# An attention and MoE chain on one core: the reciprocals are spread to the partitions in two transfers for each pair of heads

## The chip, the core and the metric

The kernel runs on one core of a Trainium2 chip. The metric is the device time of one execution in microseconds (us), as the median of several runs. One more execution was recorded by the hardware profiler; the views below are of it.

The core has five engines that run side by side, each in its own order of instructions: TensorE (PE in the views, PEld for its weight loads), VectorE (DVE), ScalarE (ACT), GpSimd (POOL) and SyncE (SP). All transfers of this kernel are issued by SP and carried by 16 DMA engines.

## The reference

Three parts follow one another. The first is a linear attention over 4 batches, 8 heads, 576 positions and 64 channels:

```
phi(x):  proj = x @ w_phi;  proj -= max(abs(proj));  concat(exp(proj), exp(-proj))
kv  = phi(k)^T v            z   = sum over s of phi(k)
num = phi(q) kv             den = phi(q) z + 1e-6
attn = num / den
```

The second is `h = x @ w_in; g = max(0.01 h, h); g @ w_out` on 2304 tokens with 512 and 2048 channels. The third is a mixture of four experts, `sum over e of p_e * (max(x @ w1_e, 0) @ w2_e)`, with normalized probabilities `p`.

## The kernel before

Heads are worked on in pairs (`hp`), so that two heads of 64 channels fill 128 partitions; a batch has four pairs. For each pair a list of steps is put out (`STEPS`, line 385): loads of `k`, `q` and `v` (lines 154, 161, 166), the features of `k` (`k_feat`), the product with `v` (`kv_side`), the projection of `q` and its absolute maximum over the partitions by GpSimd (`q_proj`, line 296, tile `mb`), the subtraction (`q_sub`, line 301), the exponentials (`q_exp`, tile `e`) and the numerator (`q_num`, line 335, copied to `nf` by ScalarE). In `nf` one row also carries the denominators, since `v` is extended by ones.

Three steps then divide. `x_den` (line 347) takes the row of denominators of each head by a small transfer to a tile `ds` of 128 partitions and 9 columns (line 352). `x_rec` (line 357) adds 1e-6 and takes the reciprocal on VectorE (lines 359 and 360), writes the 2 x 576 values to a DRAM tile `dr` (line 362), and reads them back into a tile `rb` of 128 x 576 in which each of the two rows is repeated over 64 partitions (line 364). `x_mul` (line 367) multiplies each head's half of `nf` with its half of `rb` into `xr` (line 378), and splits `xr` into a rounded part `xh` on ScalarE and a rest `xl` on VectorE (lines 117 and 118).

The second part of the reference works in units of 128 of the 2048 channels (`moe1_up`, `moe1_down`). Its matmuls need all four pairs of a batch. In the first batch the weights are also taken apart from 64 bit words: loads of 1 MB for two units (`w64_dma`, line 442), then a split by one ScalarE and several VectorE instructions (`w64_split`, lines 457 to 464 and 118), and a write of the result to DRAM (line 468) for the later batches, which load it back (line 432). The third part follows from about 650 us on.

The attention of batch `b + 1` is woven between the second part's steps of batch `b` by a table of due times (`TIMES`, with `LO` and `HI`); the first batch's attention comes ahead of everything. The order in which these functions are called isn't the final one. A scheduler orders the instructions of each engine by its own estimate of when each would be ready, up to the third part, whose instructions are kept in program order (`kept`). SP's queue too is ordered in this way. An instruction of an engine, SP's issues included, doesn't start before the one ahead of it on that engine.

Of the kernel before, what the change touches and what calls it, by code (L numbers as in the profile page):

```python
# [14 lines left out]
B, H, S, D = 4, 8, 576, 64  # L15
# [64 lines left out]
def body(ctx, tc, kT, qT, vh, w_phi, w_in, w_out, probs, w1, w2, out):  # L80
    nc = tc.nc
# [22 lines left out]
    def unit(name, dt=F32):  # L104
        return up.tile([128, S], dt, tag="u", name=name)
# [251 lines left out]
    def x_rec(b, hp):  # L357
        ds = dss[b, hp]
        nc.vector.tensor_scalar(out=ds, in0=ds, scalar1=1e-6, scalar2=None, op0=ALU.add)
        nc.vector.reciprocal(ds, ds)  # L360
        dr = drp.tile([2, S], F32, tag="dr", name="dr")
        nc.sync.dma_start(out=dr.rearrange("a (p c) -> (a p) c", c=9), in_=ds)
        rb = unit("rb")
        nc.sync.dma_start(out=rb, in_=dr.unsqueeze(1).to_broadcast([2, D, S]))
        dss[b, hp] = rb

    def x_mul(b, hp):
# [41 lines left out]
        (q_num, 1, (1,)),  # L409
        (x_den, None, ()),  # L410
        (x_rec, None, ()),
        (x_mul, None, ()),
    )
# [521 lines left out]
```

## Time and profile before

| | |
|---|---|
| median of 3 runs | 1399.87 us (1398.96 to 1400.92) |
| profiled execution | 1398.86 us, span 1397.1 us |
| TensorE busy | 1355.4 us, 97% |
| VectorE busy | 816.9 us, 58% |
| ScalarE busy | 658.4 us, 47% |
| GpSimd busy | 572.7 us, 41% |
| transfers on the hardware queue | 133.58 MB, 29.2% of 16 engines' span |

How to read the views. The page gives busy times and shares, and the span in 40 slices of about 35 us as digits (tenths). The table by stretches has a line for each stretch: its bounds in us, its length, then for PE, PEld, DVE, ACT and POOL the busy time and in brackets the number of instructions, then TensorE's granted clock as a share of 2.4 GHz, the mean share of the 16 DMA engines that is busy, and the rate in GB/s. The time line has the start in us, the duration in us, engine, line, operation, output and inputs, shapes, the number of instructions merged into the row, and in square brackets how long the engine sat idle before and what ended that. A row of SP is the issue of a transfer, not the transfer. The list of transfers gives the size of each kind.

### The profile page before, as it was taken

What the parts mean: (1) busy time and instruction counts of PE and PEld (TensorE: products, weight loads), DVE (VectorE), ACT (ScalarE), POOL (GpSimd) and SP (SyncE); (2) the same over time, 40 slices, a digit from 0 to 9 for tenths busy, and PEclk for the clock granted to TensorE, in tenths of its full rate; (3) what the DMA queues carried; (4) which work ended last, traced back from release to release, by engine and by line L of the source; (5) the groups of instructions that cost most, each with busy time, mean ns of one, the idle gap of its engine ahead of it and who ended that gap; (6) DMA issues with size and microseconds to landing.
All of it is one profiled execution on the core that took longest, in us unless ns stands there. A gap on an engine that the chain in (4) does not pass through costs nothing.

```text
span 1397.1 us, 21274 instructions
## 1 busy us (share of the span) xinstructions
PE 1355.4 (97%) x8105; PEld 1264.4 (91%) x8105; DVE 816.9 (58%) x1285; ACT 658.4 (47%) x1201; POOL 572.7 (41%) x398
## 2 busy tenths in 40 slices
PE   8769989999999999999999999999999999999998
PEld 6668989999999999998999899999999999999997
DVE  5359879877777566554454544454445544454445
ACT  5547755676566544433344433444344333333331
POOL 3123101111111000015676675667677675656551
PEclk9979999999999999999999999999999999999999
DMA  6348554333332232222211221321212131212111
GB/s 218 95 120 299 199 201 126 124 107 102 113 102 78 78 105 79 69 69 76 76 61 61 76 69 67 112 70 61 76 62 74 61 119 63 76 61 76 61 61 61
DMA packets 78038, 134.94 MB, mean 97 GB/s; under 512 B 11760, under 2 KB 22128, under 8 KB 77936
## 3 DMA queue, kind: packets, MB, share of 16 engines
q1 hardware_dynamic: 77936, 133.58, 29.2%
q8 instruction: 64, 1.05, 0.3%
q14 instruction: 38, 0.31, 0.1%
HBM read 120.30 MB, written 13.18 MB: 96 GB/s over the span
## 4 chain that ended last, share of the span: by engine, by line
PE 86%; DMA 6%; DVE 4%; issue 2%; ACT 1%; POOL 0%; SPq 0%; DVEq 0%; ACTq 0%; POOLq 0%
PE po L758 28%; PE op L535 13%; PE hp L503 12%; PE py L719 11%; PE pv L719 7%; PE px L719 7%; PE kvp L242 4%; PE nm L335 2%; DMA rb<-dr 2%; DMA qraw<-qT 2%; PE pk L204 2%; DMA w<-w 1%; DMA r<-w_in 1%; PE pq L292 1%; DVE w L461 1%
## 5 line engine op out<-in xcount | busy, mean ns | idle before, releaser
L758 PE MATMUL po<-wd,gh 128*128 128x512 f32 x1152 | 387.4, 391 | 0.9 <-POOL wd L711 0.9
L774 DVE SCALAR_TENSOR_TENSOR ob<-po,pe,ob 128x512 f32<-128x512 f32 x270 | 201.6, 749 | 216.5 <-PE po L758 216.5
L758 PEld LDWEIGHTS po<-wd,gh 128*128 128x128 f32 x1152 | 216.3, 188 | 42.5 <-POOL wd L711 1.3
L535 PE MATMUL op<-gt,wt 128*128 128x288 f32 x1536 | 222.7, 299 | 6.7 <-DVE g L517 5.3
L296 POOL PARTITION_ALL_REDUCE mb<-pc x32 | 76.9, 2406 | 370.8 <-ACT pc L294 312.6
L758 PE MATMUL po<-wd,gl 128*128 128x512 f32 x576 | 226.0, 392 | 0.0
L503 PE MATMUL hp<-xh,wt 128*128 128x288 f32 x1024 | 216.1, 298 | 3.3 <-ACT xh L117 3.3
L535 PEld LDWEIGHTS op<-gt,wt 128*128 128x128 f32 x1536 | 210.3, 190 | 8.4 <-DVE g L517 5.8
L503 PEld LDWEIGHTS hp<-xh,wt 128*128 128x128 f32 x1024 | 167.5, 188 | 4.3 <-ACT xh L117 3.6
L503 PE MATMUL hp<-xl,wt 128*128 128x288 f32 x512 | 152.2, 297 | 0.4 <-DVE xl L118 0.4
L711 POOL TENSOR_TENSOR wd<-r,wd 128x1024 fp32r<-128x1024 f32 x48 | 115.1, 2397 | 88.8 <-ACT wd L707 88.8
L719 PE MATMUL py<-xo,wuh 128*128 128x384 f32 x576 | 148.2, 338 | 0.7 <-DVE pz L824 0.7
L679 POOL TENSOR_TENSOR rs<-r 128x256 f32<-128x256 f32 x96 | 71.3, 744 | 188.1 <-DMA r<-w 188.1
L701 POOL TENSOR_TENSOR wul<-rs,wuh 128x1024 fp32r<-128x1024 f32 x48 | 115.5, 2406 | 66.2 <-ACT wuh L696 66.2
L701 POOL TENSOR_TENSOR wul<-r,wuh 128x768 fp32r<-128x768 f32 x48 | 88.9, 1851 | 84.9 <-ACT wuh L696 84.9
L758 PEld LDWEIGHTS po<-wd,gl 128*128 128x128 f32 x576 | 108.1, 188 | 15.3
L719 PEld LDWEIGHTS py<-xo,wuh 128*128 128x128 f32 x576 | 104.9, 188 | 4.6 <-DVE pz L824 1.0
L719 PE MATMUL pv<-xo,wuh 128*128 128x384 f32 x384 | 99.0, 339 | 0.0
L719 PE MATMUL px<-xo,wuh 128*128 128x384 f32 x384 | 98.6, 338 | 0.0
L503 PEld LDWEIGHTS hp<-xl,wt 128*128 128x128 f32 x512 | 96.4, 188 | 1.1 <-DVE xl L118 0.7
L719 PE MATMUL py<-xo,wul 128*128 128x384 f32 x288 | 97.2, 338 | 0.0
L804 ACT COPY py<-px 128x384 f32<-128x384 f32 x48 | 22.2, 463 | 143.6 <-PE px L719 137.5
(114 smaller groups left out, 2349.7 us busy)
## 6 DMA issues: line engine op xcount, KB each, us to landing
r<-w SPq DMA_DIRECT2D x192, 256.0 KB, 2.6
wr<-w SPq DMA_DIRECT2D x96, 256.0 KB, 3.3
qraw<-qT SPq DMA_DIRECT2D x32, 288.0 KB, 7.1
r<-w_out SPq DMA_DIRECT2D x9, 1024.0 KB, 9.0
r<-w_in SPq DMA_DIRECT2D x8, 1024.0 KB
w<-w SPq DMA_DIRECT2D x32, 256.0 KB, 2.2
v<-vh SPq DMA_DIRECT2D x16, 480.0 KB, 3.9
kraw<-kT SPq DMA_DIRECT2D x16, 288.0 KB, 5.1
```

The costliest lines, as they stand in the source:

```text
L204: nc.tensor.matmul(o, lhsT=x[:, cs], rhs=w, start=(i == 0), stop=(i == len(P) - 1))
L242: nc.tensor.matmul(kvp[:, a * 128 : (a + 1) * 128], lhsT=lhs, rhs=v[:, c, h * D : h * D + 128], start=(c == 0), stop=(c == 4),)
L296: nc.gpsimd.partition_all_reduce(mb, pc, 128, bass_isa.ReduceOp.absmax)
L335: nc.tensor.matmul(o, lhsT=a[:, 2 * (h % 2) + j], rhs=x[:, j * HS : (j + 1) * HS], start=(j == 0 and i == 0), stop=(j == 1 and i == len(P) ...
L503: nc.tensor.matmul(hp[:, n, 0:HS], lhsT=wi[:, a, kk * 128 : (kk + 1) * 128], rhs=x[z][:, kk, n * HS : (n + 1) * HS], start=(kk == 0 and i ...
L535: nc.tensor.matmul(op[:, n, 0:HS], lhsT=wt1[1, C * GF + f][:, a, d * 128 : (d + 1) * 128], rhs=gts[C * GF + f][:, z, n * HS : (n + 1) * HS ...
L679: kept(nc.gpsimd.tensor_tensor(out=o, in0=x, in1=y, op=op))
L701: kept(nc.gpsimd.tensor_tensor(out=lo[:, at], in0=(r[:, 1:4], s)[i], in1=hi[:, at].bitcast(F32), op=ALU.subtract))
L711: kept(nc.gpsimd.tensor_tensor(out=d[:, 1], in0=r2, in1=d[:, 0].bitcast(F32), op=ALU.subtract))
L719: kept(nc.tensor.matmul(out, lhsT=ws[w][:, AOPS[a], kk * 128 : (kk + 1) * 128], rhs=xo[z][:, kk], start=first and n == 0, stop=n == 5, ski ...
L758: kept(nc.tensor.matmul(op, lhsT=(gh, gl)[z][:, 2 * f + t, q : q + 128], rhs=d[:, w, f], start=n == 0, stop=n == 5,))
L774: kept(nc.vector.scalar_tensor_tensor(out=o, in0=op, scalar=ps, in1=o, op0=ALU.mult, op1=ALU.add))
```

## The change

Line 364 issues one transfer for both heads, from a source with the dimensions 2 (the rows), 64 (repeats of a row) and 576. In its place a loop over the two heads issues two transfers, each from one row, repeated 64 times, to 64 partitions.

```diff
         rb = unit("rb")
-        nc.sync.dma_start(out=rb, in_=dr.unsqueeze(1).to_broadcast([2, D, S]))
+        for o in range(2):
+            nc.sync.dma_start(
+                out=rb[o * D : (o + 1) * D], in_=dr[o : o + 1].to_broadcast([D, S])
+            )
         dss[b, hp] = rb
```

The lines behind it stand three lines further down. The numbers and shapes of all other instructions stay, but the scheduler puts them in another order in many places of the first two parts.

VectorE, where the first pair's `xr` stands, before (`ds` here is pair 1's, `mb` the subtraction for pair 1's first head, `m` and `pk` features of `k`):

```order
L378 TENSOR_TENSOR xr<-nf,rb 64x576 x2
L301 TENSOR_TENSOR mb<-pc,mb 128x576
L359 TENSOR_SCALAR ds<-ds 128x9
L118 TENSOR_TENSOR xl<-xr,xh 128x576
L360 RECIPROCAL ds<-ds 128x9
L209 TENSOR_REDUCE m<-pk 128x2
```

and now:

```order
L381 TENSOR_TENSOR xr<-nf,rb 64x576 x2
L118 TENSOR_TENSOR xl<-xr,xh 128x576
L359 TENSOR_SCALAR ds<-ds 128x9
L301 TENSOR_TENSOR mb<-pc,mb 128x576
L360 RECIPROCAL ds<-ds 128x9
L209 TENSOR_REDUCE m<-pk 128x2
```

The rest of the split (`xl`) and the add on `ds` have moved ahead of the subtraction `mb`.

SP's queue from the fetches of pair 3's denominators (`ds`) to its `rb`, before (`r_...` are the weight loads of 1 MB):

```order
L352 DMA ds<-nf 64x1x9 x2
L166 DMA qraw<-qT 128x576
L362 DMA dr<-ds 128x9
L154 DMA kraw<-kT 128x576
L364 DMA rb<-dr 128x1x576
L442 DMA r_615<-w_in 128x2x1024
L442 DMA r_627<-w_out 128x2x1024
```

and now:

```order
L352 DMA ds<-nf 64x1x9
L166 DMA qraw<-qT 128x576
L352 DMA ds<-nf 64x1x9
L154 DMA kraw<-kT 128x576
L362 DMA dr<-ds 128x9
L445 DMA r_619<-w_in 128x2x1024
L445 DMA r_631<-w_out 128x2x1024
L365 DMA rb<-dr 64x576 x2
```

Both weight loads have moved ahead of `rb`, and the second fetch behind the load of `q`.

VectorE, at pair 3's `xr`, before (`w_...` are the steps of a weight split):

```order
L301 TENSOR_TENSOR mb<-pc,mb 128x576
L276 TENSOR_TENSOR qr<-qraw,qr 64x576
L378 TENSOR_TENSOR xr<-nf,rb 64x576 x2
L216 TENSOR_TENSOR ky<-pk,m 128x256
L301 TENSOR_TENSOR mb<-pc,mb 128x576
```

and now:

```order
L216 TENSOR_TENSOR ky<-pk,m 128x512
L301 TENSOR_TENSOR mb<-pc,mb 128x576
L461 TENSOR_SCALAR w_675<-w_675 128x512
L464 SCALAR_TENSOR_TENSOR w_675<-r_619,w_675 128x512
L467 SCALAR_TENSOR_TENSOR w_675<-r_619,w_675 128x512
L381 TENSOR_TENSOR xr<-nf,rb 64x576
```

The second subtraction `mb` and three steps of a split have moved ahead of pair 3's `xr`.

## Rows read from the trace of the kernel before

**Rows 1.** The page: busy shares, and TensorE's clock in 40 slices.
```profile
PE 1355.4 (97%) x8105; PEld 1264.4 (91%) x8105; DVE 816.9 (58%) x1285; ACT 658.4 (47%) x1201; POOL 572.7 (41%) x398
...
PEclk9979999999999999999999999999999999999999
```

**Rows 2.** Table by stretches, five stretches of 50 us.
```profile
50.00:100.00 50.00, 34.13 (x165) 28.75 (x166) 21.37 (x40) 18.94 (x43) 6.85 (x3) 0.76 0.42 121
100.00:150.00 50.00, 46.90 (x323) 43.92 (x323) 47.88 (x83) 38.74 (x80) 13.51 (x4) 1.00 0.67 246
150.00:200.00 50.00, 49.73 (x355) 47.56 (x354) 44.25 (x78) 32.09 (x68) 4.28 (x2) 1.00 0.63 224
200.00:250.00 50.00, 44.57 (x322) 43.70 (x320) 42.98 (x67) 27.43 (x52) 7.20 (x3) 0.93 0.38 120
...
300.00:350.00 50.00, 50.00 (x395) 50.00 (x393) 39.81 (x60) 35.35 (x71) 8.97 (x4) 1.00 0.36 105
```

**Rows 3.** Time line of VectorE, 28 to 100 us.
```profile
32.98 0.17 DVE L359 TENSOR_SCALAR ds<-ds 128x9 f32<-128x9 f32 x1 [2.02 <-DMA ds<-nf]
...
45.57 1.52 DVE L378 TENSOR_TENSOR xr<-nf,rb 64x576 f32<-64x576 f32 x2 [5.23 <-DMA rb<-dr]
47.12 0.76 DVE L301 TENSOR_TENSOR mb<-pc,mb 128x576 f32<-128x576 f32 x1
...
61.04 0.46 DVE L273 CAST qr<-qraw 128x576 fp32r<-128x576 f32 x1 [10.89 <-DMA qraw<-qT]
...
76.30 1.52 DVE L378 TENSOR_TENSOR xr<-nf,rb 64x576 f32<-64x576 f32 x2 [9.80 <-DMA rb<-dr]
...
90.24 1.52 DVE L378 TENSOR_TENSOR xr<-nf,rb 64x576 f32<-64x576 f32 x2 [6.61 <-DMA rb<-dr]
```

**Rows 4.** Time line of SP, 28 to 105 us: issues of transfers.
```profile
30.42 0.47 SPq L352 DMA_DIRECT2D ds<-nf  x1
...
35.71 0.61 SPq L364 DMA_DIRECT2D rb<-dr  x1
...
42.40 0.48 SPq L352 DMA_DIRECT2D ds<-nf  x1
48.78 0.33 SPq L362 DMA_DIRECT2D dr<-ds  x1
...
51.52 0.42 SPq L166 DMA_DIRECT2D qraw<-qT  x1
...
65.42 0.33 SPq L362 DMA_DIRECT2D dr<-ds  x1
...
70.88 1.44 SPq L352 DMA_DIRECT2D ds<-nf  x2
...
78.30 0.33 SPq L362 DMA_DIRECT2D dr<-ds  x1
```

**Rows 5.** List of transfers, the `rb` kind: count, size of each.
```profile
rb<-dr SPq DMA_DIRECT2D x16, 288.0 KB
```

**Rows 6.** Table by stretches, four short stretches.
```profile
39.00:42.00 3.00, 3.00 (x17) 2.42 (x16) 1.31 (x2) 1.83 (x5) 2.14 (x1) 1.00 0.13 51
43.00:44.00 1.00, 1.00 (x12) 1.00 (x11) 0.00 (x0) 0.00 (x0) 1.00 (x1) 1.00 0.86 277
...
110.00:120.00 10.00, 7.36 (x44) 5.98 (x43) 8.56 (x16) 7.76 (x18) 1.46 (x1) 1.00 1.03 401
...
206.00:208.00 2.00, 0.18 (x2) 0.00 (x0) 0.00 (x0) 0.00 (x0) 0.00 (x0) 1.00 0.14 55
```

**Rows 7.** Time lines of SP, ScalarE and VectorE, 195 to 215 us.
```profile
197.35 0.54 SPq L364 DMA_DIRECT2D rb<-dr  x1
...
199.27 1.59 SPq L468 DMA_DIRECT2D w<-w  x2
...
208.75 0.66 ACT L457 ACTIVATE w<-r 128x512 f32<-128x512 f32 x1 [6.96 <-DMA w<-w]
...
209.44 0.43 DVE L458 TENSOR_SCALAR w<-w 128x512 uint32<-128x512 uint32 x1 [5.67 <-ACT w L457]
```

## The prediction

> **What bounds the kernel now.** I read the page's busy shares first: TensorE is busy 97% of the span [rows 1], so only the places where it isn't can give time. The tenths show a first place: the granted clock drops to 7 in one slice of 35 us, from 70 to 105 us [rows 1]. The table by stretches says more in numbers [rows 2]. From 300 to 350 us TensorE runs 395 matmuls in 50 us, without a gap. Between 50 and 100 us it runs 165, and over 100 to 250 us 323 + 355 + 322 = 1000, which at the later rate would need 1000 / 395 x 50 = 126.6 us and takes 150. So TensorE has 23.4 us of slack between 100 and 250 us, and more before it. VectorE is the busy one there: 47.88, 44.25 and 42.98 of 50 us. From about 91 us to 250 us VectorE sets the pace, behind the weights that it splits, and what comes before is a chain of latencies.
>
> Next the time line of VectorE before 100 us, for what it waits for [rows 3]. Four idle stretches stand out: 5.23 us until the first `rb` transfer has landed, 10.89 us until a `qraw` load has, 9.80 and 6.61 us until the third and fourth `rb` have; 32.5 us together. The `qraw` load belongs with them: it is issued at 51.52 us [rows 4], right behind the second `rb`, and lands 9.5 us later.
>
> Why a transfer of 288 KB [rows 5] takes so long is in the table by stretches again [rows 6]. From 39 to 42 us nothing but the first `rb` is in flight; the DMA share is 0.13, two of sixteen engines, and 51 GB/s move. 294,912 bytes at 51 GB/s are 5.8 us. One microsecond later, when a load that is spread over the engines runs, the share is 0.86 and the rate 277 GB/s; at that rate the same bytes need 1.1 us. A spread load behind it in the queue has its share on those two engines too, so it waits as well.
>
> **The change part by part.** It turns each of 16 transfers into two. The old source has an outer dimension of 2 (the heads), then 64 repeats, then the row; each new one has the 64 repeats outermost. I take the 64 rows of each half to be spread as a load of 128 rows is now, so both halves together need 1.1 us of data and not 5.8: 4.7 us less for each pair. No row of before shows this shape. The bounds: nothing gained (the two engines stay, 5.8 us), and 4.7 us gained; I take the 277 GB/s row, since the two engines follow the outer 2, which is gone.
>
> The Trainium skill, page "DMA: Bandwidth & Descriptors", has two rules that pull apart here. In "Rules for kernel authors" it says not to bother with two transfers to disjoint partition halves, as both halves go over all 16 engines and serialize; by that the sum would be nothing. The same table says that an outermost dimension below 16, a leading zero-stride repeat for instance, confines a DMA to that many engines; the 0.13 share agrees with it, and by it the first rule's premise (that the single transfer is already spread) fails here.
>
> The added issues cost SP about 0.55 us each [rows 4, 7], 16 x 0.55 = 8.8 us over 500 us. SP stands waiting far longer around these places (it issues nothing from 42.9 to 48.78 us, [rows 4]), so I cost them at nothing; without that cover each would push what is behind it by 0.55 us.
>
> Now the chain, pair by pair, on the times of before. The gain isn't four times the stall, because other things are late next.
>
> Pair 0: `rb` is issued at 35.71 us, and would land at 45.57 - 4.7 = 40.9 us. VectorE then takes `xr`. But in the new order the add on `ds` of pair 1 stands ahead of the subtraction `mb`, where it stood behind. That `ds` is fetched by an issue at 42.40 us [rows 4], which no `rb` holds back, and such a fetch took 2.56 us when nothing was in its way (30.42 to 32.98 us, [rows 3, 4]). So `ds` arrives at 45.0 us, `mb` starts at 45.1 instead of 47.12, and `dr` of pair 1 goes out some 2.4 us earlier than at 48.78. A stall of 5.23 us thus gives 2.4 us.
>
> Pair 1: the `qraw` load then lands at 61.04 - 2.4 - 4.7 = 53.9 us. The whole run of work behind it moves by 7.1 us, with `dr` of pair 2 at 58.3 instead of 65.42. Its `ds`, issued some 3 us earlier, arrives at about 57.6 us, just in time.
>
> Pair 2: `xr` would start at 76.30 - 7.1 - 4.7 = 64.5 us. The next late thing is again a fetch: the second `ds` of pair 3 is issued at about 71.9 us now (two issues from 70.88 on, [rows 4]), behind matmuls that move by 6.5 us with `mb`. It arrives at 65.4 + 2.5 = 67.9, and `dr` of pair 3 goes out at about 68.9 instead of 78.30: 9.4 us gained.
>
> Pair 3: the new order puts two weight loads of 1 MB each ahead of this `rb`, which stood ahead of them. From `dr` to `xr` it takes 90.24 - 78.30 = 11.9 us now. In the new order: 0.4 us to the first load's issue, 2.56 us of latency, 2.1 MB at 277 to 401 GB/s (the second from the stretch from 110 to 120 us, [rows 6]) 7.6 to 5.2 us, and 1.1 us of its own; 9.3 to 11.7, and I take 10.5. `xr` then starts at 79.4 instead of 90.24: 10.8 us. Meanwhile VectorE does one `mb` and the three steps of a weight split that now stand behind `xr`: four instructions of 0.43 to 0.76 us (ends from [rows 3, 7]), 1.7 to 3.0, taken as 2.5. So the stretch in which VectorE is the bound begins 13.3 us earlier in effect.
>
> Within that stretch one stall depends on an `rb`. At 199.27 us SP issues the write of a split weight to DRAM, behind an `rb` issued at 197.35 us; ScalarE waits 6.96 us for that write and VectorE 5.67 us for ScalarE [rows 7]. From 206 to 208 us the DMA share is 0.14 at 55 GB/s [rows 6]: the write is done but for the two engines. Spread, it lands 4.7 us sooner, and that much of VectorE's stall goes. The `rb` of later batches cost VectorE almost nothing now, and TensorE has no gap after 300 us, so I count nothing there.
>
> The sum: 13.3 + 4.7 = 18.0 us, within TensorE's slack. The profiled execution took 1398.86 us (span 1397.1), so 1380.9; the median of the runs stands 1.0 us higher, which gives 1381.9, and I say 1382. The mean clock of 0.76 from 50 to 100 us and 0.93 from 200 to 250 us [rows 2] should mostly rise with the gaps gone; VectorE is the bound behind both, so I add nothing for it.
>
> **The rivals.** *More comes back.* If the `ds` fetches arrive early too, with two engines free, all four stalls shrink to the time of a spread transfer, 4 x 2.6 us: 32.5 - 10.4 + 4.7 = 26.8 us, 1373. For it: the fetches go through the same queue. Against it: their issue waits for TensorE and ScalarE.
>
> *Less stays.* The loads of 1 MB bring the engines to a share of 1.03 at 401 GB/s from 110 to 120 us [rows 6]. If these loads and the new order after 100 us (hundreds of places move) set the pace, only about 8 of the 9.4 us that pair 3's `dr` moves remain and the rest turns into waits: 1392.
>
> *It doesn't do what it says.* The halves run on two engines as well, or one after the other: 16 issues hidden on SP, the same landings, 1400. Against it stand 0.13 and 0.86. This is the result of the skill's first rule above.
>
> *Slower.* Sixteen engines read the same 2.3 KB row of DRAM at once, and the row gives way. Now each of two engines moves 64 rows of 2,304 bytes in 5.8 us, 91 ns a row. Spread, each moves 8; from 0.73 us a row on the change loses. At 1.0 us it takes 8 us, 2.2 us more for each of the four pairs and for the write at 199 us: 1400 + 11 = 1411. Against it: two engines reading two rows run at 25 GB/s each, above the 17 GB/s that each of sixteen has at 277 GB/s, so a repeated row is not slow.
>
> **How the numbers follow.** The forecast 0.62, more 0.18, less 0.11, nothing 0.04, slower 0.05. About 0.2% (2.8 us) is what a measurement of this kernel can tell from no change. Faster has 0.62 + 0.18 + 0.11 = 0.91, same 0.04, slower 0.05. The forecast's own bounds are its terms': a dispersion of 4 us at pair 3 with its loads, 4.7 at the write, and some microseconds of new order after 100 us. The range goes from 1369, beyond "more", to 1394, beyond "less".
>
> **What would show it.** In the profile after: the DMA share nowhere at 0.13 with some 51 GB/s beside an `rb`; `xr` of pair 0 near 41 us; VectorE then waiting for `ds` and not `rb`; the `qraw` cast near 54 us; pair 3's `xr` near 79 us; no stall of over 2 us near 200 us; the clock at 2.4 GHz from some 85 us on. Wrong it would be if `xr` of pair 0 still came at 45 us (nothing), if pair 3's came after 86 us (the weight loads cost more), or if VectorE's idle time between 100 and 250 us grew by what the start gave.

## The result, and the profile after

| | before | after |
|---|---|---|
| median of 4 runs | 1399.41 us | 1380.29 us |
| lowest to highest | 1397.69 to 1400.92 | 1378.18 to 1381.59 |
| profiled span | 1397.1 us | 1378.8 us |

The ratio is 0.9863, with a 95% interval of 0.9851 to 0.9875: 19.1 us less, where 18.0 were forecast (1382 us, range 1369 to 1394).

The page after, to be held against [rows 1]: TensorE's busy time is about the same, on a span 18.3 us shorter, so what has gone is idle time and time at the lower clock.

```profile
PE 1352.1 (98%) x8105; PEld 1262.2 (92%) x8105; DVE 817.8 (59%) x1285; ACT 657.9 (48%) x1201; POOL 567.8 (41%) x398
```

The table by stretches after, for the four stretches of [rows 2] before 250 us, in which TensorE had its slack:

```profile
50.00:100.00 50.00, 40.51 (x234) 36.39 (x233) 32.95 (x54) 24.87 (x53) 10.71 (x5) 0.83 0.55 174
100.00:150.00 50.00, 48.10 (x334) 45.01 (x333) 48.17 (x85) 37.12 (x77) 7.70 (x3) 1.00 0.59 211
150.00:200.00 50.00, 50.00 (x357) 48.16 (x356) 46.35 (x82) 33.19 (x66) 2.14 (x1) 1.00 0.69 240
200.00:250.00 50.00, 49.02 (x375) 48.27 (x374) 46.41 (x73) 32.91 (x66) 9.52 (x4) 1.00 0.41 131
```

The reader is to look at VectorE, the third busy time: 32.95 us of work between 50 and 100 us where it was 21.37, and 46.41 between 200 and 250 us where it was 42.98. The clock of the last stretch is 1.00 where it was 0.93. TensorE itself is busy 48.10 + 50.00 + 49.02 = 147.1 of the 150 us from 100 to 250 us, where it was busy 141.2: little idle time is left in it there.

How far VectorE has come by a time shows where the gain lies. The same table from the start to 100 and to 250 us, first before, then after:

```profile
0.00:100.00 100.00, 75.08 (x389) 63.01 (x390) 48.22 (x83) 46.76 (x99) 22.35 (x14) 0.88 0.47 148
0.00:250.00 250.00, 216.28 (x1383) 198.20 (x1383) 183.34 (x308) 145.01 (x296) 47.34 (x23) 0.94 0.52 177
```

```profile
0.00:30.00 30.00, 23.37 (x103) 18.61 (x104) 13.96 (x24) 14.12 (x28) 7.18 (x8) 0.94 0.64 226
0.00:100.00 100.00, 83.71 (x460) 72.30 (x461) 60.74 (x98) 55.04 (x116) 26.40 (x16) 0.90 0.54 176
0.00:250.00 250.00, 230.82 (x1519) 213.75 (x1520) 201.67 (x334) 158.25 (x324) 45.76 (x24) 0.96 0.55 187
```

By 100 us VectorE is 60.74 - 48.22 = 12.5 us of work ahead, by 250 us 201.67 - 183.34 = 18.3 us, as much as the difference of the spans. Read so, the gain arises in two parts, 12.5 us before 100 us and 5.8 us between 100 and 250 us. Work done is only a rough measure of time gained (in one run below VectorE is further ahead at 250 us, and the kernel ends no earlier). The two runs that make the change in one part of the program alone measure the parts by themselves.

VectorE's time line after, for the waits of [rows 3]:

```profile
34.25 0.17 DVE L359 TENSOR_SCALAR ds<-ds 128x9 f32<-128x9 f32 x1 [2.02 <-DMA ds<-nf]
...
41.52 2.29 DVE L381 TENSOR_TENSOR xr<-nf,rb 64x576 f32<-64x576 f32 x2
...
46.18 0.17 DVE L359 TENSOR_SCALAR ds<-ds 128x9 f32<-128x9 f32 x1 [0.24 <-DMA ds<-nf]
46.26 0.75 DVE L301 TENSOR_TENSOR mb<-pc,mb 128x576 f32<-128x576 f32 x1
...
54.99 0.46 DVE L273 CAST qr<-qraw 128x576 fp32r<-128x576 f32 x1 [5.54 <-issue]
...
65.03 1.53 DVE L381 TENSOR_TENSOR xr<-nf,rb 64x576 f32<-64x576 f32 x2 [4.53 <-DMA rb<-dr]
...
69.61 0.25 DVE L359 TENSOR_SCALAR ds<-ds 128x9 f32<-128x9 f32 x1 [0.39 <-DMA ds<-nf]
...
77.77 0.43 DVE L461 TENSOR_SCALAR w<-w 128x512 uint32<-128x512 uint32 x1 [3.11 <-ACT w L460]
...
80.47 0.75 DVE L381 TENSOR_TENSOR xr<-nf,rb 64x576 f32<-64x576 f32 x1 [0.82 <-DMA rb<-dr]
```

The first wait for `rb` is gone, the wait at the `qraw` cast is 5.54 us where it was 10.89 (put down to "issue", since the profile shows nothing that ended it; the load was issued 5.2 us before), the next 4.53 where it was 9.80. Ahead of pair 3's `xr` the engine now waits for the weights (3.11 us) and then 0.82 us for `rb`. New are the two short waits for `ds`, 0.24 and 0.39 us.

The issues on SP after, for [rows 4]:

```profile
36.83 1.10 SPq L365 DMA_DIRECT2D rb<-dr  x2
...
43.60 0.47 SPq L352 DMA_DIRECT2D ds<-nf  x1
47.16 0.33 SPq L362 DMA_DIRECT2D dr<-ds  x1
...
49.81 0.52 SPq L166 DMA_DIRECT2D qraw<-qT  x1
...
59.42 0.33 SPq L362 DMA_DIRECT2D dr<-ds  x1
...
70.61 0.33 SPq L362 DMA_DIRECT2D dr<-ds  x1
70.99 0.43 SPq L445 DMA_DIRECT2D r<-w_in  x1
```

This execution is 1.3 us late from its first 30 us on: its first `ds` add starts at 34.25 and not 32.98 us, and the clock's mean over the first 30 us is 0.94 here, where it was 1.00 before:

```profile
0.00:30.00 30.00, 23.39 (x108) 18.70 (x109) 15.96 (x25) 15.51 (x31) 8.26 (x8) 1.00 0.67 234
```

In the two runs below that keep the order of instructions this add starts at 32.63 and 32.81 us, so the lateness belongs to this execution and not to the change. 1.3 us have to be taken off before a time is held against one of before; counted in, they make VectorE 12.5 + 1.3 = 13.8 us ahead at 100 us.

The transfers, and the stretch that showed two engines in [rows 6], after:

```profile
rb<-dr SPq DMA_DIRECT2D x32, 144.0 KB, 3.6
```

```profile
39.00:40.00 1.00, 1.00 (x6) 0.79 (x5) 0.88 (x1) 0.17 (x1) 0.00 (x0) 1.00 0.96 277
40.00:41.00 1.00, 1.00 (x6) 0.79 (x5) 0.97 (x2) 0.91 (x2) 0.00 (x0) 1.00 0.36 97
41.00:42.00 1.00, 1.00 (x6) 0.79 (x5) 1.00 (x2) 0.43 (x2) 0.88 (x1) 1.00 0.00 0
```

The last column but one is the share of the 16 engines: nearly all are busy until 40 us, and at 41 us nothing is in flight. There is no tail at 0.13.

### The profile page after: what moved, and what is told of

Its sections match the earlier page's. It is cut to its first block, busy times and chain, and to the rows that moved or that the text cites. A ratio compares the mean times of both kernels' runs of the same rounds, so it can differ in the third digit from the quotient of the medians.

```text
span 1378.8 us, 21301 instructions
## 1 busy us (share of the span) xinstructions
PE 1352.1 (98%) x8105; PEld 1262.2 (92%) x8105; DVE 817.8 (59%) x1285; ACT 657.9 (48%) x1201; POOL 567.8 (41%) x398
## 4 chain that ended last, share of the span: by engine, by line
PE 95%; DVE 1%; DMA 1%; issue 1%; ACT 1%; POOL 1%; SPq 0%; POOLq 0%; ACTq 0%; DVEq 0%
PE po L761 29%; PE hp L506 15%; PE op L538 14%; PE py L722 11%; PE pv L722 7%; PE px L722 7%; PE kvp L242 5%; PE nm L335 4%; PE pk L204 2%; PE pq L292 1%; PE pq L289 1%; DMA qraw<-qT 1%; POOL wul L704 0%; DMA r<-w 0%; DMA ds<-nf 0%
## 5 line engine op out<-in xcount | busy, mean ns | idle before, releaser
L538 PE MATMUL op<-gt,wt 128*128 128x288 f32 x1536 | 219.9, 297 | 1.5 <-DVE gt L118 0.8
L296 POOL PARTITION_ALL_REDUCE mb<-pc x32 | 72.3, 2266 | 355.7 <-ACT pc L294 294.7
```

The lines of the kernel that those rows point to most:

```text
L296: nc.gpsimd.partition_all_reduce(mb, pc, 128, bass_isa.ReduceOp.absmax)
L538: nc.tensor.matmul(op[:, n, 0:HS], lhsT=wt1[1, C * GF + f][:, a, d * 128 : (d + 1) * 128], rhs=gts[C * GF + f][:, z, n * HS : (n + 1) * HS ...
```

## The experiments

Medians and ratios are against the kernel before, run on the same chip in turn. Its median was 1399.41 us beside the changed kernel, 1398.5 us beside the first four runs here and 1399.78 us beside the last three, so a difference between runs of different groups can be off by about 1 us from that alone.

**The same order, two engines.** The outer dimension of each half's source is made 2. All five engines have the same order of instructions as in the changed kernel.

```diff
-                out=rb[o * D : (o + 1) * D], in_=dr[o : o + 1].to_broadcast([D, S])
+                out=rb[o * D : (o + 1) * D],
+                in_=dr[o : o + 1].to_broadcast([2, S]).unsqueeze(1).to_broadcast([2, D // 2, S]),
```

> Two transfers as in the changed kernel, and the same order of instructions on all five engines, but each half's source has an outer dimension of 2 over 32 repeats of the row. Theory (the engines that carry a transfer make the time): DMA share near 0.13 again beside rb, xr of pair 0 near 45 to 46 us, 1395 to 1405 us. Rival (the new order of instructions, or the split itself, makes the time): 1378 to 1384 us, as the changed kernel.

Measured: 1406.16 us, ratio 1.0051 (1.0033 to 1.0068), 1.2 us above the theory's range and far above the rival's. The table of stretches and VectorE's time line of this kernel:

```profile
39.00:42.00 3.00, 3.00 (x19) 2.53 (x19) 1.55 (x2) 1.83 (x5) 2.14 (x1) 1.00 0.14 47
```

```profile
44.97 0.76 DVE L382 TENSOR_TENSOR xr<-nf,rb 64x576 f32<-64x576 f32 x1 [3.01 <-DMA rb<-dr]
...
60.59 0.46 DVE L273 CAST qr<-qraw 128x576 fp32r<-128x576 f32 x1 [11.10 <-issue]
...
211.14 0.43 DVE L462 TENSOR_SCALAR w<-w 128x512 uint32<-128x512 uint32 x1 [5.93 <-ACT w L461]
```

The share is back at 0.14, the second half of `rb` is waited for at 45 us, and the stalls of 11 and 6 us are there again. So the split alone gives nothing: with two engines it is even 7.7 us slower (1406.16 against 1398.5), and the source's outer dimension alone, at the same order, is worth 1406.16 - 1380.29 = 25.9 us. Little of those 7.7 us is lost before 250 us. By then TensorE has run 1379 matmuls where it had run 1383 before, and VectorE 182.66 us of work where it had 183.34; by 300 us TensorE has run 1717 where it had run 1768. Most of the loss stands in a gap of TensorE and the low clock after it:

```profile
250.00:255.00 5.00, 2.24 (x12) 1.44 (x11) 4.97 (x9) 4.09 (x8) 0.56 (x1) 0.92 0.64 209
255.00:260.00 5.00, 5.00 (x21) 5.00 (x22) 4.91 (x7) 2.33 (x6) 2.36 (x1) 0.50 0.56 195
```

12 and 21 matmuls in 5 us each, where before the same stretches had 35 and 41. VectorE is busy throughout, and TensorE waits 1.67 and 0.70 us for its results. The order of VectorE's work differs there from before, but the order alone doesn't make the gap: at the same order and with sixteen engines TensorE is idle for only 1.0 us between 200 and 300 us. A late `rb` stands ahead of the gap, too; the wait for it was 0.84 us at this place before, and from here to the gap VectorE is hardly idle:

```profile
239.90 0.76 DVE L382 TENSOR_TENSOR xr<-nf,rb 64x576 f32<-64x576 f32 x1 [2.08 <-DMA rb<-dr]
```

How the two share the gap, and which instruction of the order it hangs on, wasn't tried.

**The same order, four engines.** The same edit with 4 in place of 2.

> As the run before, but with an outer dimension of 4 over 16 repeats. Theory: four engines carry 32 rows each, 2.9 us of data in place of 5.8 (two) and about 1 (all), so some 60% of the gain: 1385 to 1391 us, and a DMA share of 0.25 beside a lone rb. Rival (order or split): 1378 to 1384 us.

Measured: 1385.84 us, ratio 0.9908 (0.9893 to 0.9923). The stretch in which `rb` is alone, and the wait at the `qraw` cast:

```profile
39.00:40.00 1.00, 1.00 (x6) 0.79 (x5) 0.94 (x1) 0.75 (x2) 0.56 (x1) 1.00 0.26 78
```

```profile
55.31 0.46 DVE L273 CAST qr<-qraw 128x576 fp32r<-128x576 f32 x1 [7.54 <-issue]
```

0.26 is four engines of sixteen. At one order of instructions two, four and sixteen engines give 1406.2, 1385.8 and 1380.3 us. By the rate on two engines (5.8 us for a pair) and the 1.1 us of the spread, an estimate, the first step saves 2.9 us of data for each pair and 20.3 us of time, the second some 1.8 us and 5.5 us: the time falls with the transfer at each step, but not in proportion, since with two engines the gap after 250 us comes on top.

**The first batch only.**

```diff
+        if b > 0:
+            nc.sync.dma_start(out=rb, in_=dr.unsqueeze(1).to_broadcast([2, D, S]))
+        else:
+            for o in range(2):
...
```

> Only the four transfers of the first batch are made in two; the twelve later ones stay as before. Theory (13.3 us come from the start of the program, 4.7 us from the stall near 200 us): 1384 to 1389 us, with an idle stretch of VectorE of some 5 us near 190 us left. Rival (all of the gain is at the start): 1379 to 1382 us.

Measured: 1385.02 us, ratio 0.9904 (0.9889 to 0.9919), 13.5 us less than before. The late stall is left, at 193 to 199 us and as long as expected:

```profile
198.67 0.43 DVE L464 TENSOR_SCALAR w<-w 128x512 uint32<-128x512 uint32 x1 [5.57 <-ACT w L463]
```

**The later batches only.** The reverse (`if b == 0` keeps the one transfer).

> Only the twelve transfers of the later batches are made in two; the first batch's four stay as before. Theory: 1393 to 1397 us, the four idle stretches of VectorE before 100 us as before, no stall of over 2 us near 200 us. Rival (all of the gain is at the start): 1398 to 1401 us.

Measured: 1392.64 us, ratio 0.9957 (0.9942 to 0.9972), 5.9 us less and 0.4 us below the theory's range. The early waits are as before, and the late one has shrunk:

```profile
59.93 0.46 DVE L273 CAST qr<-qraw 128x576 fp32r<-128x576 f32 x1 [10.79 <-DMA qraw<-qT]
...
202.38 0.43 DVE L464 TENSOR_SCALAR w<-w 128x512 uint32<-128x512 uint32 x1 [1.83 <-ACT w L463]
```

The two parts, 13.5 and 5.9 us, add up to 19.4, against 19.1 for the whole change. Each of these figures has an interval of some 2 us to either side, so this shows no more than that neither part needs the other to within a few microseconds.

**`rb` of pair 3 ahead of the weight loads.** The weight loads for the second pair of units are kept behind what SP was given before.

```diff
+    last = {}
...
-            nc.sync.dma_start(
+            last["rb"] = nc.sync.dma_start(
...
-        nc.sync.dma_start(
+        ins = nc.sync.dma_start(
...
+        if last and f == 2:
+            tc.keep_in_program_order(ins)
```

> The changed kernel, with the two 1 MB weight loads of the first groups kept behind pair 3's rb on SP, as they stood before; the scheduler then moves other instructions as well. Theory (behind the loads rb needs 9.9 us from dr to xr, ahead of them some 5.1): xr of pair 3 starts at 75 to 77 us, the weights land 1.5 us later, and the stretch where VectorE is the bound starts up to 3 us earlier: 1376 to 1380 us. Rival (VectorE has to wait for the weights there anyway, so the place of rb is worth nothing): 1380 to 1383 us.

Measured: 1380.02 us, ratio 0.9857 (0.9841 to 0.9872); no difference from the changed kernel, and on the border of the two ranges. VectorE's time line:

```profile
33.22 0.17 DVE L360 TENSOR_SCALAR ds<-ds 128x9 f32<-128x9 f32 x1 [2.15 <-DMA ds<-nf]
...
74.87 0.75 DVE L382 TENSOR_TENSOR xr<-nf,rb 64x576 f32<-64x576 f32 x1 [1.81 <-DMA rb<-dr]
...
80.33 0.43 DVE L464 TENSOR_SCALAR w<-w 128x512 uint32<-128x512 uint32 x1 [0.72 <-ACT w L463]
```

The first `ds` add shows that this execution isn't late as that of the changed kernel is (33.22 and not 34.25 us). With these 1.0 us added, `xr` starts 4.6 us earlier than at 80.47, and the weight split 3.6 us later than at 77.77. The landing of `rb` was as the theory had it; that it would be worth up to 3 us was wrong, and the rival's figure holds. VectorE does get ahead in this run:

```profile
0.00:100.00 100.00, 84.27 (x474) 72.65 (x474) 64.68 (x101) 57.24 (x122) 26.81 (x16) 0.95 0.60 197
0.00:250.00 250.00, 231.05 (x1533) 213.62 (x1534) 205.59 (x337) 160.30 (x327) 46.58 (x24) 0.98 0.56 187
```

It has done 64.68 us of work by 100 us and 205.59 by 250 us, 3.9 us more than in the changed kernel at both, of which 1.0 us is the late start there. TensorE gains nothing from it: from 100 to 250 us it runs 1533 - 474 = 1059 matmuls, and in the changed kernel, where it is busy 147.1 of 150 us, 1519 - 460 = 1059 as well. So after the change VectorE no longer sets the pace of that stretch alone. This is read from the rows; no run tests it.

**Four transfers for each pair.** `for o in range(4)`, each with 32 partitions.

> Four transfers of 32 partitions for each pair, in place of two of 64: 32 issues more on SP, the same bytes and the same 16 engines. Theory (SP's issues are hidden but for 1.1 us ahead of the qraw load of pair 1 and on each rb's own landing in the first batch): 1380 to 1385 us. Rival (each issue of 0.55 us is paid): 32 x 0.55 = 17.6 us, 1395 to 1400 us.

Measured: 1378.44 us, ratio 0.985 (0.9834 to 0.9867), 1.6 us below the theory's range. SP's and VectorE's rows for pair 1:

```profile
46.03 1.71 SPq L365 DMA_DIRECT2D rb<-dr  x4
```

```profile
52.13 0.46 DVE L273 CAST qr<-qraw 128x576 fp32r<-128x576 f32 x1 [4.74 <-DMA qraw<-qT]
```

Four issues take 1.7 us and not 2.2, and nothing of them is seen in the time: 32 more issues cost nothing that can be measured, and the rival of 17.6 us has fallen. Its order of instructions differs too; its interval overlaps that of the changed kernel, so it isn't shown to be faster.

**The first batch's halves issued by ScalarE.** `nc.scalar.dma_start` in place of `nc.sync.dma_start` where `b == 0`.

> The changed kernel, with the first batch's eight halves issued by ScalarE and not by SP. Theory (landing, not issuing, matters, and ScalarE comes to these issues later, behind copies and exponentials that wait themselves): pair 0's xr some 3 us later than 41.5 us, 1381 to 1388 us. Rival (on SP they lose time behind the v loads and weight loads of the same queue, another queue saves it): 1375 to 1379 us.

Measured: 1379.93 us, ratio 0.9857 (0.984 to 0.9873). The issue on ScalarE, and VectorE's first `ds` add and pair 0's `xr`:

```profile
39.90 1.13 ACTq L365 DMA_DIRECT2D rb<-dr  x2
```

```profile
33.02 0.17 DVE L359 TENSOR_SCALAR ds<-ds 128x9 f32<-128x9 f32 x1 [2.12 <-DMA ds<-nf]
...
42.86 2.54 DVE L381 TENSOR_TENSOR xr<-nf,rb 64x576 f32<-64x576 f32 x2 [2.56 <-DMA rb<-dr]
```

The execution of the changed kernel is 1.2 us late against this one, by the first `ds` add. With these added the issue comes 4.3 us later than at 36.83 and `xr`, which waits for it, 2.6 us later than at 41.52, about as expected. Yet the time is that of the changed kernel: 1 us below the theory's range, above the rival's. Neither was right. A landing that is a few microseconds later or earlier no longer changes the time measurably, in this run and in the one with `rb` ahead of the weights.

## Why the prediction was right, point by point

**Two engines, then all.** Shown by the runs with 2 and 4 as the outer dimension: 0.14, 0.26 and no such tail, at one order of instructions. The rule of the Trainium skill ("DMA: Bandwidth & Descriptors", "Rules for kernel authors") that an outermost dimension below 16 confines a transfer to at most that many engines agrees with these shares. The one against two transfers to partition halves doesn't hold where the one transfer has an outer dimension of 2: 1380.29 against 1399.41 us.

**The chain of pairs.** Less the 1.3 us by which this execution is late, the times after stand beside the forecast so:

| step | forecast | measured, less 1.3 |
|---|---|---|
| `mb` of pair 1 | 45.1 | 45.0 |
| `dr` of pair 1 | 46.4 | 45.9 |
| `qraw` cast | 53.9 | 53.7 |
| `dr` of pair 2 | 58.3 | 58.1 |
| `xr` of pair 2 | 64.5 | 63.7 |
| `dr` of pair 3 | 68.9 | 69.3 |
| `xr` of pair 3 | 79.4 | 79.2 |

What made this come out is that each stall removed was followed up to what is late next: VectorE does wait for `ds` at 46.18 and 69.61 us, by 0.24 and 0.39 us, where it would otherwise have gone on. At pair 3 two small errors cancel: `dr` goes out 0.4 us later than forecast, and from `dr` to `xr` it takes 9.9 us and not 10.5.

**The two terms.** 13.3 us before 100 us: VectorE is 12.5 us ahead there (13.8 without the late start), and the first batch alone gives 13.5. I let the stretch in which VectorE is the bound begin with pair 3's `xr`. That is right in size here, where `rb` lands right behind the weights, but not as a rule: with `rb` ahead of the weights `xr` came 4.6 us earlier and the kernel no sooner. 4.7 us near 200 us: 5.8 us by VectorE's work, and 5.9 by the later batches alone. The second is the one mis-sized term, about 1 us too small, which is within the interval of that run. Around the place itself the waits are short now; rows of ScalarE and VectorE after, to hold against [rows 7]:

```profile
191.33 0.67 ACT L460 ACTIVATE w<-r 128x512 f32<-128x512 f32 x1 [1.16 <-DMA w<-w]
```

```profile
192.03 0.43 DVE L461 TENSOR_SCALAR w<-w 128x512 uint32<-128x512 uint32 x1 [1.07 <-ACT w L460]
```

5.67 - 1.07 = 4.6 us of VectorE's longest stall, as forecast. The rest I had counted at nothing; VectorE waited for the same kind of ScalarE instruction at other places between 90 and 250 us as well, and these waits, the longest among them, sum to 2.5 us now where they were 10.2.

**SP's issues at nothing.** Borne out, and with 32 issues more as well.

**The clock.** It was said to be at 2.4 GHz from some 85 us on. It came back a little later: TensorE still has a gap at 75 us, where VectorE waits for the weights.

```profile
75.00:80.00 5.00, 1.31 (x7) 1.01 (x5) 1.81 (x3) 1.16 (x3) 0.00 (x0) 0.50 0.88 344
80.00:85.00 5.00, 3.35 (x12) 3.02 (x13) 4.47 (x9) 3.29 (x7) 0.00 (x0) 0.50 0.35 117
85.00:90.00 5.00, 5.00 (x33) 5.00 (x33) 5.00 (x9) 1.82 (x3) 0.00 (x0) 0.72 0.29 107
```

The mean from 85 to 90 us is 0.72, so somewhat more than half of that stretch is still at 1.2 GHz. The sum had nothing for the clock. In the run with `rb` ahead of the weights its mean over the first 100 us is 0.95 where it is 0.90 in the changed kernel, and the time is the same.

**The rivals.** "More comes back" fell by the waits for `ds`, and "less stays" by the 5.8 us gained after 100 us. "Slower", by sixteen engines that read one row at once, fell too: with sixteen `rb` was the quickest of the three. "More comes back" is also refuted by the time, 19.1 us and not 26.8. The split without the spread is what "it doesn't do what it says" described, at 1400 us and with the time of before; built as an experiment it took 1406.2 us, so its cost was put too low there.

**What stays open.** What the new order of instructions costs or gives by itself under a spread transfer. With two engines the new order is 7.7 us slower than the old one, most of it after 250 us, and what makes that gap isn't shown. The one move of it that was undone, the weight loads ahead of `rb`, is worth nothing.

## What to carry to other kernels

Where a transfer of a few hundred kilobytes takes ten microseconds, look at the share of engines while it is alone: 0.13 is two of sixteen, as many as the outer dimension of the source. Then follow the stall to what is late next before you count it: 32.5 us of idle time held 13.5 us of gain here. A transfer on few engines also delays what is queued behind it, so part of the gain can lie far away, as at the write near 200 us.

## What the runs showed of the hardware that wasn't expected

Four issues of the same kind in a row took SP 1.71 us, 0.43 us each, where two took 1.10 us and one alone 0.54 to 0.61 us. And a row of 2.3 KB in DRAM can be read by sixteen engines at once: the halves land 3.6 us (median) after their issue, with the wait behind other loads in it.
